# Converting float64 weights inside an attention and expert kernel: an integer sum in place of a float product

## The chip, the cores and the metric

The kernel runs on one core of one Trainium2 chip. The metric is device time in microseconds (us). Before the change three runs gave 2444.08, 2444.11 and 2446.53 us; the median is 2444.11 us.

## What is computed

Top-k attention over 4 batches, 8 heads, 576 rows of 64 (the 32 largest scores of a row are kept), then a bilinear layer, then eight experts weighted by a gate that is normalised eight times. The part that matters here is the layer in the middle:

```python
def _moe_ref(x, w1, w2, w3, w_out):
    a = x @ w1
    b = x @ w2
    h = a * b @ w3
    return (h @ w_out).astype(np.float32)
```

Its four weights are drawn as float32 and divided by a numpy float64 scalar, so they reach the kernel as 64-bit floats. The chip's engines work on 32-bit numbers, so the kernel has to make float32 out of float64 bits itself: sign, exponent and the first mantissa bits lie in the top 16-bit word, the rest in the words below it.

## The kernel before

**The attention stage** is a loop of 72 steps (`for s in range(NS + 6)`, L615). In step s VectorE finds the 32 largest scores of two rows of tiles (`st_topk`, L214): four rounds of MAX8 (L221) with three rounds of MATCH_REPLACE8 (L227) between. ScalarE evicts scores of step s+1 (L202), masks and exponentiates step s-1 (L234, L246), and evicts the transposed probabilities and the attention output of step s-2 (L270, L304). GpSimd normalises (L261), TensorE does the products. Every engine runs its instructions in the order in which the program wrote them, so one that waits holds up all that stands behind it on its engine.

**The conversion** of the four weights is woven into the first 23 steps: 40 pieces of 128x512 numbers, 8 of `w_out`, then 16 of `w3` with 8 of `w1` among them, then 8 of `w2`. A piece goes through `cv_run` (L341). `run_cv` (L556) calls it at two places in a step, after the second transposition and at the end of the step. There ScalarE computes two candidates `ca` and `cb` from the top word (L351, L352), and, for `w_out` alone, scales the low 32-bit word (L356). VectorE's part is put into `dve_q`, from which `st_topk` takes one entry at each of its seven slots (`dve_slot`) in the next step: `c1` chooses between the candidates and writes the top half of the float (L359, into `Q`), `c2` keeps sign and exponent (L363), `c3` multiplies these by the low word (L373; for `w_out` GpSimd does it, L371). GpSimd then adds `Q` and the product (L376, L378). For `w1` and `w2` the sum is split into a high and a low part for the later products: `hi` on ScalarE (L334), `lo` on GpSimd (L335), by `cv_flush`, in the middle of the same step.

**The raw pieces** come by DMA from SP's queue into `raw`, which has three buffers (`RB`). `cv_next` (L327) issues the load of piece n+3 as soon as the program has written `c3` of piece n, since no later instruction reads the raw words.

**w_out and w3** are multiplied with each other first: TensorE transposes a `w3` piece (L442), ScalarE copies it out (`w3t`, L443), TensorE multiplies it with `wo` (`wps`, L451), ScalarE evicts (L453). These items follow in the step after the piece was converted.

**After the `w1` pieces** (`NCA` = 32 of them done) the pools are closed and new ones opened for `w2` (`wt_close`, L422); `cb` then has one buffer instead of two. When all 40 pieces are done, `moe1_pool` opens the buffers of the middle layer and its products (L492, L510) are dealt out over the steps up to the next batch: step 37 for the first batch. The number of steps left sets how many products a step gets (`per`, L625). After the 72 steps come the experts (L690 on), where TensorE is busy throughout.

Of the kernel before, what the change touches and what calls it, by code (L numbers as in the profile page):

```python
# [7 lines left out]
F32 = mybir.dt.float32  # L8
F32R = mybir.dt.float32r
U16 = mybir.dt.uint16  # L10
U32 = mybir.dt.uint32
AF = mybir.ActivationFunctionType
ALU = mybir.AluOpType
AX = mybir.AxisListType
# [3 lines left out]
def kernel(  # L18
# [14 lines left out]
    nc = tc.nc  # L33
# [15 lines left out]
    scale = 1.0 / float(D) ** 0.5  # L49
# [65 lines left out]
    split = {}  # L115

    def copy(dst, src, eng):
        if eng is None:
            nc.scalar.activation(dst, src, AF.Copy)
        else:  # L120
            eng.tensor_copy(dst, src)

    def prep_split(p, nm, eng=nc.gpsimd):
        src = nat.pop((nm, p))
        hl = ap1.tile([128, 2 * R + 1, 2, D], F32R, name=f"{nm}hl", tag=f"{nm}hl")
        nc.scalar.activation(hl[:, :, 0, :], src, AF.Copy)
        eng.tensor_tensor(hl[:, :, 1, :], src, hl[:, :, 0, :].bitcast(F32), ALU.subtract)
# [58 lines left out]
    def st_scores(st, j):  # L186
# [13 lines left out]
        if j == 0:  # L200
            s_sb[st] = ap1.tile([128, 2, S], F32, name="s_sb", tag="s_sb", bufs=3)
        nc.scalar.activation(s_sb[st][:, j].rearrange("p (a b) -> p a b", a=2), ps[:, :, 0:SH], AF.Copy,  # L202
                             scale=scale)

    dve_q = []
# [25 lines left out]
    def st_over(st, j):  # L231

        x = s_sb[st][:, j]
        nc.scalar.activation(x, x, AF.Prelu, bias=tkv[st][:, j, TOPK - 1:TOPK], scale=-1.0, alpha=2.0 ** -100)  # L234

# [5 lines left out]
    def st_exp(st, j):  # L241
        if j == 0:
            e_sb[st] = ap1.tile([128, 2, S], F32, name="e_sb", tag="e_sb", bufs=2)
            rden[st] = ap1.tile([128, 2], F32, name="rden", tag="rden", bufs=2)
        rd = rden[st]
        nc.scalar.activation(e_sb[st][:, j], s_sb[st][:, j], AF.Exp, bias=nbias[st][:, j:j + 1],  # L246
                             scale=-(2.0 ** 100), accum_out=rd[:, j:j + 1])
        if j:
            nc.scalar.activation(rd, rd, AF.Identity, bias=eps)
            nbias.pop(st)  # L250
# [56 lines left out]
    CW = 512  # L307
    RB = 3
# [4 lines left out]
    cv = {"p": cvx.enter_context(tc.tile_pool(name="cv", bufs=1, side="left")), "n": 0}  # L313
    w3r = {}
    raws = {}
    gsc = G.rearrange("p f t -> p (f t)")
# [3 lines left out]
    nc.gpsimd.memset(gsc[:, 0:2 * CW], 0.0)  # L320

    def cv_load(key, src):
        t = cv["p"].tile([128, 4 * CW + 4], U16, name="raw", tag="raw", bufs=RB)
        nc.sync.dma_start(t[:, 1:4 * CW + 1], src.bitcast(U16))
        raws[key] = t

    def cv_next(n):  # L327
        if n < len(cvs) and not n - 3 < NCA <= n:
            cvs[n][1]()

    cv_post = []

    def hi_lo(w, hi, lo):
        nc.scalar.activation(hi, w, AF.Copy)  # L334
        nc.gpsimd.tensor_tensor(lo, w, hi.bitcast(F32), ALU.subtract)  # L335
# [5 lines left out]
    def cv_run(key, dst, done=None):  # L341
        t = raws.pop(key)
        pos = cpos[0]
        y = t[:, 4:4 * CW + 4].rearrange("p (n f) -> p n f", f=4)[:, :, 0]
        rest = t.bitcast(U32)[:, 0:2 * CW].rearrange("p (n f) -> p n f", f=2)[:, :, 1]
        n, m = cv["n"] % 2, cv["n"] % 3
        cv["n"] += 1
        Q = gsc[:, CW * n:CW * n + CW]
        ca = gsc[:, CW * (2 + m):CW * (3 + m)]
        cb = cv["p"].tile([128, CW], F32, name="cb", tag="cb", bufs=1 if "w2" in m1p else 2)  # L350
        nc.scalar.activation(ca, y, AF.Relu, bias=cbias[:, 0:1], scale=8.0)  # L351
        nc.scalar.activation(cb, y, AF.Identity, bias=cbias[:, 1:2], scale=8.0)  # L352

        off = key[0] == "o"
        if off:
            nc.scalar.activation(rest.bitcast(F32), rest, AF.Copy, scale=2.0 ** -36)  # L356

        def c1():
            nc.vector.scalar_tensor_tensor(Q.bitcast(U16).rearrange("p (n f) -> p n f", f=2)[:, :, 1],  # L359
                                           ca, 32768.0, cb, op0=ALU.min, op1=ALU.max)  # L360

        def c2():
            nc.vector.tensor_scalar(ca.bitcast(U32), Q.bitcast(U32), 0xff800000, None, op0=ALU.bitwise_and)  # L363

        def c23():
            c2()
            c3()

        def c3():
            if off:  # L370
                nc.gpsimd.tensor_tensor(ca, rest.bitcast(F32), ca, ALU.mult)  # L371
            else:
                nc.vector.scalar_tensor_tensor(ca, rest, 2.0 ** -36, ca, op0=ALU.mult, op1=ALU.mult)  # L373
            cv_next(pos + 3)
            if key[0] in ("o", "3"):
                nc.gpsimd.tensor_tensor(dst(), Q, ca, ALU.add)  # L376
            else:
                nc.gpsimd.tensor_tensor(ca, Q, ca, ALU.add)  # L378
                cv_post.append(lambda: hi_lo(ca, *dst()))
            if done is not None:  # L380
                done()

        dve_q.extend([c1, c23] if off else [c1, c2, c3])

    def cv_list():
        r = []

        def add(key, src, dst, done=None):
            r.append((key, lambda: cv_load(key, src), lambda: cv_run(key, dst, done)))

        def w3dst(i, hf):
            w3r[i, hf] = wtp.tile([128, CW], F32, name="w3r", tag="w3r", bufs=4)
            return w3r[i, hf]

        def wdst(n, c, sl):
            hi, lo = (w1h, w1l) if n == 0 else m1p["w2"]
            return hi[:, c, sl], lo[:, c, sl]

        for i in range(FC):
            add(("o", i), w_out[128 * i:128 * i + 128, :], lambda i=i: wo[:, i])  # L400
        def add3(i, hf):
            add(("3", i, hf), w3[128 * i:128 * i + 128, CW * hf:CW * hf + CW], lambda: w3dst(i, hf),
                lambda: later(1, w_items(i, hf)))

        def add12(n, c, hf):
            sl = slice(CW * hf, CW * hf + CW)
            add((n, c, hf), (w1, w2)[n][128 * c:128 * c + 128, sl], lambda: wdst(n, c, sl))

        k3 = [(i, hf) for i in range(FC) for hf in range(2)]
        k1 = [(c, hf) for c in range(KD) for hf in range(2)]  # L410
        for n, k in enumerate(k3):
            add3(*k)
            if n % 3 == 2:
                add12(0, *k1.pop(0))
        for k in k1:
            add12(0, *k)
        for c in range(KD):
            for hf in range(2):
                add12(1, c, hf)
        return r  # L420

    def wt_close():  # L422
        cvx.close()
        wt.close()
        m1p["w2p"] = wab.enter_context(tc.tile_pool(name="w2p", bufs=1, side="left", reuse_waits="tile"))
        m1p["w2"] = [m1p["w2p"].tile([128, KD, F1], F32R, name=n) for n in ("w2h", "w2l")]
        cvx2 = ExitStack()
        cv["p"] = cvx2.enter_context(tc.tile_pool(name="cv2", bufs=1, side="left", reuse_waits="tile"))
        m1p["cvx2"] = cvx2

    m1p = {}
# [123 lines left out]

    def run_cv():  # L556
        n = cpos[0]
        if n >= len(cvs) or sum(f is not None for f in dve_q) > 3:
            return
        key, _, fn = cvs[n]  # L560
        if key[0] == "3" and len(w3r) >= 4 and list(w3r)[-4] not in w3done:
            return
        if n == NCA and "w2" not in m1p:
            if dve_q or cv_post or fill or later_q or (FC - 1, 1) not in w3done:
                return
            wt_close()
            for i in range(3):
                cvs[n + i][1]()
            return
        if key not in raws:  # L570
            return
        fn()
        cpos[0] = n + 1
    load_pair(0)
    cvs = cv_list()
    cpos = [0]
    NCA = len(cvs) - FC
# [17 lines left out]
    st_scores(0, 0)  # L595
    st_scores(0, 1)
    run_cv()
    prep_group(0, "q", 2)
    run_cv()
    first = [9 * p // 2 for p in range(NPAIR + 1)]  # L600
    prep, loads = {}, {}
# [13 lines left out]
    for s in range(NS + 6):  # L615
# [52 lines left out]
        if 0 < s and cpos[0] < len(cvs):  # L668
            run_cv()
# [376 lines left out]
```

## Time and profile before

| | |
|---|---|
| median of three runs | 2444.11 us |
| span of the profiled execution | 2442.0 us |
| what lies around the span (median less span) | 2.1 us |
| TensorE busy | 2288.3 us, 94% of the span |
| VectorE busy | 1958.9 us, 80% |
| ScalarE busy | 1256.2 us, 51% |
| GpSimd busy | 1343.2 us, 55% |
| chain that ended last | TensorE 80%, VectorE 11%, ScalarE 5%, GpSimd 2% |

The page lists the time of no single execution beside its profile, so the span stands for it and the 2.1 us are taken as fixed. Shares over the whole span mix two halves: up to about 800 us the attention stage, after it the experts. In a timeline a row gives the start, the length, the engine, the line, what is written and read, and in brackets how long the engine had been idle and who ended that. PE is TensorE, PEld its weight load, DVE is VectorE, ACT is ScalarE, POOL is GpSimd, SP issues the DMAs. An ACT or DVE instruction begins while the end of the one before still drains, so the time that one takes of its engine is the distance to the next start, not its length.

### The profile page before, as it was taken

How to read it: one execution, taken by the hardware profiler on the slowest of the kernel's cores; microseconds unless marked ns; L12 is line 12 of the kernel's file. 1: busy time of each engine (PE TensorE's matmuls, PEld its weight loads, DVE VectorE, ACT ScalarE, POOL GpSimd, SP SyncE). 2: the span in 40 equal slices, each digit the busy share in tenths (PEclk: the TensorE clock that was granted, in tenths of full speed). 3: DMA queues.
4: the chain of work that ended last, by engine and by line, in shares of the span. 5: the costliest groups of instructions: out<-in, count | busy, mean ns of one | idle time of the engine just before them, and what ended most of it. 6: DMA issues, size and time to landing. Idle time of an engine off the chain costs nothing.

```text
span 2442.0 us, 37866 instructions
## 1 busy us (share of the span) xinstructions
PE 2288.3 (94%) x13061; PEld 2002.0 (82%) x13061; DVE 1958.9 (80%) x3560; ACT 1256.2 (51%) x2725; POOL 1343.2 (55%) x1377
## 2 busy tenths in 40 slices
PE   4677699899899999999999999999999999999999
PEld 3454489789788888889999988888888899999998
DVE  7998999999999228887777778777777777777776
ACT  6686777777777333444443444443444443444342
POOL 4534443233332125686666668666666666666664
PEclk7898789999999999999999999999999999999999
DMA  4332211111110132222222232222222322222221
GB/s 132 111 97 77 85 35 44 41 45 36 49 32 11 46 116 66 74 82 69 65 67 70 70 100 83 67 63 70 69 69 62 95 70 69 69 63 68 70 70 52
DMA packets 173296, 166.59 MB, mean 68 GB/s; under 512 B 19632, under 2 KB 137392, under 8 KB 173104
## 3 DMA queue, kind: packets, MB, share of 16 engines
q1 hardware_dynamic: 173104, 164.17, 22.4%
q8 instruction: 103, 1.69, 0.3%
q14 instruction: 89, 0.73, 0.1%
HBM read 145.24 MB, written 9.44 MB: 63 GB/s over the span
## 4 chain that ended last, share of the span: by engine, by line
PE 80%; DVE 11%; ACT 5%; POOL 2%; issue 2%; DMA 1%; SPq 0%; POOLq 0%; DVEq 0%; ACTq 0%
PE y L933 31%; PE l1ps L866 27%; PE abps L492 8%; PE x2ps L510 4%; DVE tkv L221 4%; DVE tk L227 3%; PE xps L300 3%; PE sps L198 2%; PE tps L267 2%; PE wps L451 1%; DVE G L359 1%; PE pt L137 1%; ACT e_sb L246 1%; ACT et L270 1%; ACT s_sb L202 1%
## 5 line engine op out<-in xcount | busy, mean ns | idle before, releaser
L730 POOL TENSOR_TENSOR wal<-ws,wah 128x256 fp32r<-128x256 f32 x665 | 553.9, 840 | 482.7 <-ACT wah L729 471.7
L946 DVE SCALAR_TENSOR_TENSOR acc<-y,P,acc 128x512 f32<-128x512 f32 x540 | 402.4, 745 | 215.0 <-PE y L933 214.0
L729 ACT ACTIVATE wah<-ws 128x256 fp32r<-128x256 f32 x672 | 276.3, 413 | 521.2 <-PE l1ps L866 514.9
L933 PE MATMUL y<-wbh,hh 128*128 128x512 f32 x1152 | 456.3, 396 | 4.5 <-ACT hh L887 4.5
L933 PE MATMUL y<-wbl,hh 128*128 128x512 f32 x1152 | 454.6, 395 | 0.0
L933 PE MATMUL y<-wbh,hl 128*128 128x512 f32 x1152 | 449.1, 390 | 1.9 <-DVE hl L890 1.4
L723 DVE TENSOR_TENSOR ws<-ws 128x256 f32<-128x256 f32 x384 | 319.0, 832 | 2.4 <-DMA ws<-in_moe_w_dram 1.8
L221 DVE MAX8 tkv<-tk 128x8 f32<-128x576 f32 x432 | 305.8, 752 | 0.0
L866 PE MATMUL l1ps<-xo0h,wah 128*128 128x384 f32 x896 | 304.6, 340 | 0.0
L866 PE MATMUL l1ps<-xo0h,wal 128*128 128x384 f32 x896 | 302.7, 338 | 0.0
L866 PE MATMUL l1ps<-xo0l,wah 128*128 128x384 f32 x896 | 302.7, 338 | 0.0
L933 PEld LDWEIGHTS y<-wbl,hh 128*128 128x128 f32 x1152 | 216.0, 188 | 52.7
L887 ACT ACTIVATE hh<-u 128x384 fp32r<-128x384 f32 x192 | 100.9, 525 | 297.0 <-DVE u L879 297.0
L933 PEld LDWEIGHTS y<-wbh,hl 128*128 128x128 f32 x1152 | 216.8, 188 | 30.3 <-DVE hl L890 5.8
L933 PEld LDWEIGHTS y<-wbh,hh 128*128 128x128 f32 x1152 | 216.6, 188 | 28.9 <-ACT hh L887 6.2
L738 POOL TENSOR_TENSOR wbl<-ws,wbh 128x1024 fp32r<-128x1024 f32 x96 | 231.8, 2414 | 12.5 <-ACT wbh L737 4.3
L227 DVE MATCH_REPLACE8 tk<-tkv,tk 128x576 f32<-128x576 f32 x288 | 212.4, 747 | 0.0
L866 PEld LDWEIGHTS l1ps<-xo0l,wah 128*128 128x128 f32 x896 | 169.2, 189 | 16.3
L866 PEld LDWEIGHTS l1ps<-xo0h,wah 128*128 128x128 f32 x896 | 168.9, 189 | 16.0 <-DVE hl L890 0.9
L501 POOL TENSOR_TENSOR G<-a_sb 128x256 f32<-128x256 f32 (+1 forms) x64 | 52.3, 817 | 227.4 <-ACT a_sb L497 211.6
L866 PEld LDWEIGHTS l1ps<-xo0h,wal 128*128 128x128 f32 x896 | 168.7, 188 | 0.0
L879 DVE TENSOR_TENSOR u<-l1ps,u 128x384 f32<-128x384 f32 x288 | 157.2, 546 | 4.8 <-PE l1ps L866 3.0
(146 smaller groups left out, 4912.2 us busy)
## 6 DMA issues: line engine op xcount, KB each, us to landing
ws<-in_moe_w_dram SPq DMA_DIRECT2D x384, 128.0 KB, 2.3
ws<-in_moe_w_dram SPq DMA_DIRECT2D x96, 512.0 KB, 3.5
raw<-in_moe_w_dram SPq DMA_DIRECT2D x32, 512.0 KB, 3.7
kst<-kst SPq DMA_DIRECT2D x30, 288.0 KB, 4.0
xr<-x2s SPq DMA_DIRECT2D x12, 384.0 KB, 3.6
xr<-x2s SPq DMA_DIRECT2D x6, 768.0 KB, 4.7
kn<-in_k_dram SPq DMA_DIRECT2D x16, 256.0 KB, 2.7
qn<-in_q_dram SPq DMA_DIRECT2D x16, 256.0 KB, 2.8
```

Of the source, the lines that this page charges most:

```text
L221: nc.vector.max(vt[:, j, 8 * r:8 * r + 8], a[j] if r else s[j])
L227: nc.vector.match_replace(a[j], vt[:, j, 8 * r:8 * r + 8], a[j] if r else s[j], -3.0e38)
L492: nc.tensor.matmul(ps[:, 0:n], lhs[:, c, fs], rhs[:, c, 0:n], start=(c == 0 and j == 0), stop=(c == KD - 1 and j == 2))
L723: nc.vector.tensor_tensor(st[:, dst], st[:, x], st[:, y], op)
L729: nc.scalar.activation(hi, st[:, slot], AF.Copy)
L730: eng.tensor_tensor(lo, st[:, slot], hi.bitcast(F32), ALU.subtract)
L738: nc.gpsimd.tensor_tensor(lo, st, hi.bitcast(F32), ALU.subtract)
L866: nc.tensor.matmul(ps[:, 0:TH], lhs[:, c], rhs[:, slot, c], start=(k_ == 0), stop=(k_ == 3 * KH - 1))
L879: nc.vector.tensor_tensor(t[nm], ps, t[x], ALU.add)
L887: nc.scalar.activation(t["hh"][:, i, h], src, AF.Relu)
L933: nc.tensor.matmul(ps, lhs[:, m, h, o:o + 128], rhs[:, m], start=(k_ == 0), stop=(k_ == 5))
L946: nc.vector.scalar_tensor_tensor(a, ps, P[:, t, e:e + 1], a, op0=ALU.mult, op1=ALU.add)
```

## The change

The float32 bits are put together as integers. ScalarE rounds the low word of every piece to an int32 (scaled by 2^-13, written back over the raw words as `low`), VectorE makes the top half with `c1` alone, and GpSimd adds `Q` and `low` as int32. `c2` and `c3` go, and so does GpSimd's product for `w_out`. For `w1` and `w2` the sum is written back into the raw buffer, and `hi` and `lo` read it there; so `cv_next` now stands behind `lo` for these, and behind GpSimd's sum for the others. In the `w2` part `cb` has two buffers again, and `raw` two (`RB - 1`). The candidates `ca` have two buffers instead of three.

```diff
     def cv_next(pos):
-        if n < len(cvs) and not n - 3 < NCA <= n:
+        n = pos + (RB if pos < NCA else RB - 1)
+        if n < len(cvs) and not pos < NCA <= n:
             cvs[n][1]()
...
-        n, m = cv["n"] % 2, cv["n"] % 3
+        n = cv["n"] % 2
-        ca = gsc[:, CW * (2 + m):CW * (3 + m)]
-        cb = cv["p"].tile([128, CW], F32, name="cb", tag="cb", bufs=1 if "w2" in m1p else 2)
+        ca = gsc[:, CW * (2 + n):CW * (3 + n)]
+        cb = cv["p"].tile([128, CW], F32, name="cb", tag="cb", bufs=2)
...
-        off = key[0] == "o"
-        if off:
-            nc.scalar.activation(rest.bitcast(F32), rest, AF.Copy, scale=2.0 ** -36)
+        low = rest.bitcast(I32)
+        nc.scalar.activation(low, rest, AF.Copy, scale=2.0 ** -13)
+
+        def split():
+            hi_lo(rest.bitcast(F32), *dst())
+            cv_next(pos)
...
         def c1():
             nc.vector.scalar_tensor_tensor(Q.bitcast(U16)..., ca, 32768.0, cb, op0=ALU.min, op1=ALU.max)
-        def c2():
-            nc.vector.tensor_scalar(ca.bitcast(U32), Q.bitcast(U32), 0xff800000, None, op0=ALU.bitwise_and)
-        def c3():
-            if off:
-                nc.gpsimd.tensor_tensor(ca, rest.bitcast(F32), ca, ALU.mult)
-            else:
-                nc.vector.scalar_tensor_tensor(ca, rest, 2.0 ** -36, ca, op0=ALU.mult, op1=ALU.mult)
-            cv_next(pos + 3)
             if key[0] in ("o", "3"):
-                nc.gpsimd.tensor_tensor(dst(), Q, ca, ALU.add)
+                nc.gpsimd.tensor_tensor(dst().bitcast(I32), Q.bitcast(I32), low, ALU.add)
+                cv_next(pos)
             else:
-                nc.gpsimd.tensor_tensor(ca, Q, ca, ALU.add)
-                cv_post.append(lambda: hi_lo(ca, *dst()))
+                nc.gpsimd.tensor_tensor(low, Q.bitcast(I32), low, ALU.add)
+                cv_post.append(split)
-        dve_q.extend([c1, c23] if off else [c1, c2, c3])
+        dve_q.append(c1)
...
     def run_cv():
-        if n >= len(cvs) or sum(f is not None for f in dve_q) > 3:
+        if n >= len(cvs) or len(dve_q) > 1:
...
-            for i in range(3):
+            for i in range(RB - 1):
                 cvs[n + i][1]()
```

How the instructions stand. On VectorE, in step 6, which converts two pieces (`tkv` are the maxima, `tk` the score tiles, `s_sb` the fresh scores; line numbers of the changed kernel are a few higher); before:

```order
120 L359 SCALAR_TENSOR_TENSOR G<-G,cb 128x512
121 L227 MATCH_REPLACE tk_769<-tkv,s_sb 128x576
122 L227 MATCH_REPLACE tk_770<-tkv,s_sb 128x576
123 L363 TENSOR_SCALAR G<-G 128x512
124 L221 MAX tkv<-tk_769 128x8
125 L221 MAX tkv<-tk_770 128x8
126 L373 SCALAR_TENSOR_TENSOR G<-raw,G 128x512
127 L227 MATCH_REPLACE tk_769<-tkv,tk_769 128x576
128 L227 MATCH_REPLACE tk_770<-tkv,tk_770 128x576
129 L359 SCALAR_TENSOR_TENSOR G<-G,cb 128x512
```

and on the same engine in the same step after the change:

```order
103 L222 MAX tkv<-s_sb 128x8
104 L256 RECIPROCAL rden<-rden 128x2
105 L222 MAX tkv<-s_sb 128x8
106 L364 SCALAR_TENSOR_TENSOR G<-G,cb 128x512
107 L228 MATCH_REPLACE tk_752<-tkv,s_sb 128x576
108 L228 MATCH_REPLACE tk_753<-tkv,s_sb 128x576
109 L364 SCALAR_TENSOR_TENSOR G<-G,cb 128x512
110 L222 MAX tkv<-tk_752 128x8
111 L222 MAX tkv<-tk_753 128x8
112 L228 MATCH_REPLACE tk_752<-tkv,tk_752 128x576
```

The second piece's `c1` moves from the fourth slot to the second, where the first piece's `c2` stood.

On ScalarE, at the middle and the end of step 18, the first that splits `w2` pieces (`et`, `xT` belong to the attention), before:

```order
312 L270 ACTIVATE et<-tps 128x640
313 L351 ACTIVATE G<-raw,cbias 128x512
314 L352 ACTIVATE cb<-raw,cbias 128x512
315 L334 ACTIVATE w2h<-G 128x512 x2
316 L304 ACTIVATE xT<-xps 128x128
317 L351 ACTIVATE G<-raw,cbias 128x512
318 L352 ACTIVATE cb<-raw,cbias 128x512
```

and after the change, from the same place on:

```order
338 L271 ACTIVATE et<-tps 128x640
339 L337 ACTIVATE w2h<-raw 128x512 x2
340 L305 ACTIVATE xT<-xps 128x128
341 L354 ACTIVATE G<-raw,cbias 128x512
342 L355 ACTIVATE cb<-raw,cbias 128x512
343 L357 ACTIVATE raw<-raw 128x512
344 L235 ACTIVATE s_sb<-s_sb,tkv 128x576 x2
```

With two raw buffers one piece instead of two is begun in this step, and its three instructions stand close behind the `hi` rows that read the raw words of the two before it. The `w2` pieces are chosen on VectorE in steps 18 to 21, two a step, before, and in steps 18 to 22, as 2, 1, 2, 1 and 2, after. Up to step 17 the pieces stand in the same steps in both kernels, and TensorE's rows are the same.

## Rows read from the trace of the kernel before

**Rows 1.** The page's first line.
```profile
span 2442.0 us, 37866 instructions
```
**Rows 2.** Timeline of VectorE in step 5, which converts two pieces.
```profile
77.64 0.74 DVE L221 MAX8 tkv<-s_sb 128x8 f32<-128x576 f32 x1
...
81.29 0.41 DVE L363 TENSOR_SCALAR G<-G 128x512 uint32<-128x512 uint32 x1
81.62 1.41 DVE L221 MAX8 tkv<-tk 128x8 f32<-128x576 f32 x2
82.95 0.67 DVE L373 SCALAR_TENSOR_TENSOR G<-raw,G 128x512 f32<-128x512 uint32 x1
83.54 0.08 DVE L227 MATCH_VALUE_LOAD tk<-tkv,tk 128x8 f32 x1
...
85.00 0.74 DVE L359 SCALAR_TENSOR_TENSOR G<-G,cb 128x512 uint16<-128x512 f32 x1
...
90.67 0.74 DVE L221 MAX8 tkv<-s_sb 128x8 f32<-128x576 f32 x1
```
**Rows 3.** Timeline of VectorE in a step without conversion.
```profile
636.85 0.76 DVE L221 MAX8 tkv<-s_sb 128x8 f32<-128x576 f32 x1
...
646.56 0.75 DVE L221 MAX8 tkv<-s_sb 128x8 f32<-128x576 f32 x1
```
**Rows 4.** Stretches: length, busy PE, PEld, DVE, ACT, POOL (instructions), clock, DMA, GB/s.
```profile
77.09:249.98 172.89, 130.82 (x735) 82.65 (x736) 159.68 (x325) 122.74 (x245) 70.48 (x72) 0.89 0.30 94
261.38:313.80 52.42, 33.05 (x164) 25.65 (x164) 52.42 (x104) 37.84 (x76) 24.45 (x24) 0.58 0.23 68
322.69:462.21 139.52, 138.92 (x1142) 125.90 (x1141) 136.97 (x296) 106.70 (x241) 46.81 (x66) 0.99 0.15 42
```
**Rows 5.** Waits of ScalarE, 77 to 250 us: us in total, times, longest.
```profile
ACT et L270 <- PE tps L268: 19.6, 8, 4.9
ACT xT L304 <- PE xps L300: 19.0, 8, 6.1
ACT G L351 <- POOL w1l L335: 5.4, 3, 4.7
...
ACT s_sb L234 <- DVE tkv L221: 1.1, 1, 1.1
```
**Rows 6.** Waits of VectorE, 77 to 250 us.
```profile
DVE G L359 <- ACT cb L352: 9.0, 5, 2.6
```
**Rows 7.** Timeline of ScalarE, end of step 7.
```profile
115.54 0.59 ACT L443 ACTIVATE w3t<-pt 128x512 f32<-128x512 f32 x1
121.09 0.28 ACT L304 ACTIVATE xT<-xps 128x128 f32<-128x128 f32 x1 [4.95 <-PE xps L300]
```
**Rows 8.** Timeline of TensorE, the same place.
```profile
116.19 3.61 PE L451 MATMUL wps<-wo,w3t 128*128 128x512 f32 x4 [3.87 <-ACT w3t L443]
```
**Rows 9.** ScalarE's scaling of the low word, by line: ns min/median/max.
```profile
L356 ACT ACTIVATE raw<-raw x8: 646/662/713, 17.9 to 61.4; 128x512 f32<-128x512 uint32 x8
```
**Rows 10.** Timeline of ScalarE in steps 6 and 8, from the split on.
```profile
104.13 0.62 ACT L334 ACTIVATE w1h<-G 128x512 fp32r<-128x512 f32 x1
104.64 0.59 ACT L453 ACTIVATE W<-wps 128x512 f32<-128x512 f32 x1
...
106.13 0.77 ACT L351 ACTIVATE G<-raw,cbias 128x512 f32<-128x512 uint16 x1 [0.18 <-POOL w1l L335]
...
137.25 0.28 ACT L304 ACTIVATE xT<-xps 128x128 f32<-128x128 f32 x1 [0.45 <-PE xps L300]
```
**Rows 11.** GpSimd's low part by line, and the raw loads' time to landing.
```profile
L335 POOL TENSOR_TENSOR w1l<-G,w1h x8: 1256/1275/1368, 104.8 to 249.2; 128x512 fp32r<-128x512 f32 x8
...
DMA to landing us min/median/max: 3.2/3.7/5.4
```
**Rows 12.** Timeline of VectorE and of GpSimd in step 19.
```profile
272.77 1.75 DVE L359 SCALAR_TENSOR_TENSOR G<-G,cb 128x512 uint16<-128x512 f32 x1
...
271.43 2.50 POOL L335 TENSOR_TENSOR w2l<-G,w2h 128x512 fp32r<-128x512 f32 x2
```

More of the change, by code (lines that the diff above doesn't have):

```diff
@@ L11 @@
 U32 = mybir.dt.uint32
+I32 = mybir.dt.int32
 AF = mybir.ActivationFunctionType
@@ L322, in cv_load, with cv_next @@
     def cv_load(key, src):
-        t = cv["p"].tile([128, 4 * CW + 4], U16, name="raw", tag="raw", bufs=RB)
+        t = cv["p"].tile([128, 4 * CW + 4], U16, name="raw", tag="raw",
+                         bufs=RB - 1 if "w2" in m1p else RB)
         nc.sync.dma_start(t[:, 1:4 * CW + 1], src.bitcast(U16))
         raws[key] = t
-    def cv_next(n):
-        if n < len(cvs) and not n - 3 < NCA <= n:
+    def cv_next(pos):
+        n = pos + (RB if pos < NCA else RB - 1)
+        if n < len(cvs) and not pos < NCA <= n:
             cvs[n][1]()
@@ L360, in c1 @@
                                            ca, 32768.0, cb, op0=ALU.min, op1=ALU.max)
-        def c2():
-            nc.vector.tensor_scalar(ca.bitcast(U32), Q.bitcast(U32), 0xff800000, None, op0=ALU.bitwise_and)
-        def c23():
-            c2()
-            c3()
-        def c3():
-            if off:
-                nc.gpsimd.tensor_tensor(ca, rest.bitcast(F32), ca, ALU.mult)
-            else:
-                nc.vector.scalar_tensor_tensor(ca, rest, 2.0 ** -36, ca, op0=ALU.mult, op1=ALU.mult)
-            cv_next(pos + 3)
-            if key[0] in ("o", "3"):
-                nc.gpsimd.tensor_tensor(dst(), Q, ca, ALU.add)
-            else:
-                nc.gpsimd.tensor_tensor(ca, Q, ca, ALU.add)
-                cv_post.append(lambda: hi_lo(ca, *dst()))
+            if key[0] in ("o", "3"):
+                nc.gpsimd.tensor_tensor(dst().bitcast(I32), Q.bitcast(I32), low, ALU.add)
+                cv_next(pos)
+            else:
+                nc.gpsimd.tensor_tensor(low, Q.bitcast(I32), low, ALU.add)
+                cv_post.append(split)
             if done is not None:
                 done()
-        dve_q.extend([c1, c23] if off else [c1, c2, c3])
+        dve_q.append(c1)
     def cv_list():
```

## The prediction

> **What bounds the kernel now.** I began with the span [rows 1] and then asked the attention stage, in which the conversion sits, step by step. The first look is VectorE's timeline. A step that converts two pieces runs from 77.64 to 90.67, 13.03 us [rows 2]; a step that converts nothing takes 9.71 us [rows 3]. The reader is to see that VectorE goes from row to row without a gap, and that the difference of 3.3 us is the conversion. Read alone this says: VectorE is the bound, so take work off it.
>
> The second look is at stretches [rows 4]. From step 5 to step 17 (77.09 to 249.98) ScalarE was busy 122.74 of 172.89 us. That seems slack. The third look, who waited for whom, says otherwise: of ScalarE's 50 us of idle time there only 1.1 us was a wait for VectorE [rows 5]. Nearly all is for TensorE, in two forms of eight times each, up to 6.1 us. And VectorE itself waited 9.0 us for ScalarE's candidates `cb` [rows 6]. So ScalarE runs behind VectorE through these steps, and its waits are not VectorE's doing.
>
> The fourth look shows what they are. ScalarE copies `w3t` out at 115.54 and then has nothing to do until 121.09, when it gets `xps` [rows 7]. TensorE meanwhile had sat idle for 3.87 us, waiting for exactly that copy, and then took 3.61 us for four products [rows 8]. ScalarE and TensorE hand the work to and fro; when one works on this chain the other stands. In steps 5 to 16 this chain, 173 us for 12 steps, sets the pace as much as VectorE does. A faster VectorE cannot shorten it; more ScalarE work lengthens it.
>
> **The change part by part.**
>
> *VectorE.* `c2` takes 0.33 us (81.29 to 81.62) and `c3` 0.59 (82.95 to 83.54) [rows 2]. 40 x 0.33 + 32 x 0.59 = 32.1 us less. That is the whole prize, and it is only paid where VectorE sets the end. In steps 0 to 4 it nearly does. There mostly `w_out` pieces are converted, which lose `c2` alone, and the first two pieces wait for their loads. I take -1 us, between -4 and 0.
>
> *The second `c1` earlier.* It moves to the second slot. The fourth is 7.36 us into a step (85.00), the second 3.65 us (81.29) [rows 2]. Its candidates come from the end of ScalarE's step before, so VectorE now tolerates 3.7 us less of ScalarE's lag. It costs nothing of its own; it is what makes VectorE wait for the chain in every step rather than in five.
>
> *ScalarE.* One rounding more for each `w3`, `w1` and `w2` piece. The nearest row is the scaling of the same words, 0.66 us long [rows 9]. ScalarE's instructions overlap by 0.1 (a `hi` of 0.62 begins 0.51 before the next) [rows 10], so I take 0.56; an int32 output could change that, I allow 0.4 to 0.8. Between step 5 and step 16 there are 21 of them, 11.8 us, on the chain. Some fall into a wait for TensorE in which TensorE isn't waiting for ScalarE, such as the 0.45 us at 137.25 [rows 10]; I count five such places and 2.5 us in all, between 0 and 5. **+9.3 us.**
>
> *The raw buffer is held longer.* For a `w1` piece the load of the piece three later now waits for `lo`. From the start of `hi` that is 0.62 [rows 10], then 1.27 for `lo` and 3.7 for the landing [rows 11]: 5.6 us. The `w1` pieces of steps 6, 8, 10, 12 and 14 are each the first of their pair, so the piece three later is the one ScalarE takes at the end of the same step. In step 6 it gets there 2.0 us after `hi` (104.13 to 106.13) [rows 10]. It will stand 3.6 us. The same for steps 8 and 10: 10.8 us. In step 12 ScalarE already waits 4.7 us at this place, for a candidate's buffer that GpSimd still reads [rows 5]; two early `c1` free that, so 3.6 takes the place of 4.7, -1.1. In step 14 the wait of 6.1 us for `xps` [rows 5] covers it. **+9.7 us**, between 0 (loads land early) and 15. On SP the loads behind such a wait are those of later pairs' keys, queries and values, needed steps later; nothing.
>
> *GpSimd.* One product less for `w_out`, the additions as integers. No row shows an integer addition there; at half or at twice the 1.27 us of the nearest row, `lo` [rows 11], it would still be done well before ScalarE, some 6 us into its step, reaches `hi`. Nothing.
>
> So the chain reaches step 18 later by -1 + 9.3 + 9.7 = 18 us.
>
> *Steps 18 to 22, `w2`.* Now two raw buffers, and each step's last piece is loaded into the buffer that the `hi` rows just before it have to leave. ScalarE's own work from step 18's start to step 22's was 37.84 us of 52.42 [rows 4]. After: six roundings more, two `hi` fewer by step 22, 37.84 + 6 x 0.56 - 2 x 0.51 = 40.2 us. In each of the four steps it stands for the refill: 5.6 us from `hi`, less what it still does meanwhile, 1.2 us with two `hi` and 0.7 with one, so 4.4 or 4.9, twice each, 18.6 us. Together 58.8, 6.4 more. At the end VectorE gains: it began step 23 at 322.69, 8.9 us after that stretch. Now the last `c1` starts 0.6 us before the stretch ends, and 9.71 + 2 x 0.64 - 3.65 = 7.3 us of its step are left, so 6.7 us, 2.2 less (a `c1` of 0.74 takes 0.64). **+4.2 us**, between -10 (no refill wait) and +7.
>
> *One step later.* The last piece is finished in step 22, so the middle layer's products begin in step 24 instead of 23 and still end at step 37: 13 steps for the work of 14. TensorE was busy 138.92 of 139.52 us there [rows 4], so a step is 9.9 us and has no room. About half of it belongs to the layer; that half has to go elsewhere. Bounds 0 and 5; **+4 us**, near the upper one since TensorE is full.
>
> Sum: 18 + 4.2 + 4 = 26.2 us. On the span 2468.2; with 2.1 us around it, which puts the profiled execution at the median of the three runs, 2470.3, say **2470 us**.
>
> **A rule to weigh.** A `c1` of 0.74 us took 1.75 at 272.77 while GpSimd worked from 271.43 to 273.93 [rows 12]. It seems to have stood until GpSimd's instruction ended. The Trainium skill, in SBUF — State Buffer, Who interferes with whom, says that a VectorE instruction with two SBUF inputs contends with a GpSimd instruction that reads SBUF, and that the later one fully blocks. The trace agrees, with 1.0 us. My sum has none of it, since VectorE waits for ScalarE anyway.
>
> **Rivals.**
>
> *A: VectorE is the bound after all and ScalarE keeps up.* For it: no gaps in most steps [rows 2]. The price is the whole 32.1 us, less 4 for the later start: 2444.1 - 28.1 = 2416 us. It decides if ScalarE's chain shrinks by a quarter when VectorE runs ahead. Against it: ScalarE's work alone, 122.7 + 21 x 0.56 = 134.5 us, would have to go through 12 steps of VectorE of 9.71 + 1.28, 132 us, without a single wait. Chance 0.07.
>
> *B: as A, but the second `c1` is blocked.* It now comes when GpSimd adds the first piece. By the 1.0 us of rows 12, in 18 steps with two pieces, up to 18 us are given back, half of that if GpSimd has got through half its addition: 2425 us. The rule of the Trainium skill above, in SBUF — State Buffer, would make this, not A, the case. Chance 0.06.
>
> *C: the loads come in time.* SP, GpSimd and the DMA answer faster than 5.6 us, or ScalarE gets there later. Then the roundings count, the buffer waits of 5.4 us [rows 5] go, and steps 18 to 22 are VectorE's: 8 pieces x 0.92, and three blocked `c1` of 1.0, -10.4. -1 + 9.3 - 5.4 - 10.4 + 4 = -3.5: 2441 us, no change. Against it: landing never took under 3.2 us [rows 11]. Chance 0.12.
>
> *D: TensorE slows as well.* While it waits its granted clock falls: 0.89 on average in steps 5 to 16, 0.58 in the `w2` stretch [rows 4]. Of its two levels, 1.2 and 2.4 GHz, the lower would make products last twice as long; four products that took 3.61 us after an idle time of 3.87 [rows 8] would then have been 1.8. If longer waits put seven more handovers there, 7 x 1.8 = 12.6 us: 2483 us. Chance 0.15.
>
> **How the numbers follow.** The forecast has 0.60. Its own range, from the bounds of the roundings, the refills and the later start, is 2452 to 2484. A measurement of this kernel can tell about 0.2% from no change, 4.9 us: 2439.2 to 2449.0 is the same. Faster: A, B and a little of C, 0.14. Same: the rest of C and the forecast's lowest edge, 0.12. Slower: 0.74. The range reaches down to take in C and up to take in D: 2437 to 2486; A, B and the far ends, 2 in 10, are left out.
>
> **What would show it.** ScalarE's waits: a new kind, `ca` on the DMA of `raw`, of 3 to 5 us, some seven times from step 6 on, with L270's and L304's waits for TensorE much as before. VectorE's waits for `cb` far above 9 us over the same steps. Step 18 starting some 15 us later, step 23 some 22 later, the step of 9.71 unchanged where nothing is converted, the experts shifted and not stretched. I am wrong if VectorE's steps 5 to 15 take about 11 us each (A), if ScalarE never waits for `raw` (C), or if the products of L451 get slower (D).

## The result, and the profile after the change

The changed kernel took 2477.39 us (median of 4 runs, 2475.37 to 2478.79) against 2445.30 us for the kernel before (4 runs): 1.0129 times as long, 95% interval 1.0115 to 1.0143, 32 us slower. The profiled execution took 2477.46 us, 1.8 us of it around the span. The page's first lines:

```profile
span 2475.7 us, 37823 instructions
...
PE 2299.4 (93%) x13061; PEld 2010.7 (81%) x13061; DVE 1924.0 (78%) x3488; ACT 1274.4 (51%) x2757; POOL 1334.2 (54%) x1369
```

VectorE is busy 34.9 us less than before (1958.9), and the span is 33.6 us longer (unrounded) [rows 1]. The groups by line, up to 400 us, say what became of the time (busy, mean ns of one, idle time ahead of them):

```profile
L364 DVE SCALAR_TENSOR_TENSOR G<-G,cb 128x512 uint16<-128x512 f32 x40 | 35.0, 876 | 72.7 <-ACT cb L355 72.6
L354 ACT ACTIVATE G<-raw,cbias 128x512 f32<-128x512 uint16 x40 | 30.6, 764 | 37.1 <-DMA raw<-in_moe_w_dram 32.6 <-DMA raw<-in_moe_w_out_dram 4.5
...
L357 ACT ACTIVATE raw<-raw 128x512 int32<-128x512 uint32 x40 | 26.7, 668 | 0.0
L370 POOL TENSOR_TENSOR raw<-G,raw 128x512 int32<-128x512 int32 x16 | 20.6, 1290 | 21.7 <-DVE G L364 18.8 <-ACT raw L357 2.1 <-ACT s_sb L235 0.8
```

and the first of them in the kernel before:

```profile
L359 DVE SCALAR_TENSOR_TENSOR G<-G,cb 128x512 uint16<-128x512 f32 x40 | 34.9, 873 | 12.2 <-ACT cb L352 12.2
```

The 40 `c1` now stand for 72.6 us and wait for ScalarE's `cb`; before it was 12.2. VectorE saved 34.9 us of work and got 60.4 us of waiting for it. The second line after the change shows a wait that the kernel before hardly had: ScalarE's `ca` on the load of `raw`, 32.6 us for `w3`, `w1` and `w2`.

The stretches, cut by ScalarE's steps as before (steps 5 to 16, steps 18 to 21; the last is VectorE's steps 23 to 36), answer to [rows 4]:

```profile
76.60:271.75 195.15, 140.03 (x736) 87.71 (x737) 139.22 (x284) 134.22 (x266) 68.23 (x72) 0.84 0.26 77
282.59:342.14 59.55, 29.80 (x173) 23.40 (x173) 43.86 (x91) 39.87 (x80) 25.67 (x27) 0.71 0.25 78
349.30:493.66 144.36, 141.54 (x1129) 128.13 (x1126) 137.74 (x296) 106.00 (x238) 51.81 (x68) 0.97 0.14 39
```

They are longer by 22.3, 7.1 and 4.8 us. In the first, ScalarE's own work grew by 11.5 us and VectorE's busy time fell from 159.68 to 139.22.

ScalarE's waits from 77 to 272 us, which answer to [rows 5], and then those from 283 to 342:

```profile
ACT et L271 <- PE tps L269: 21.4, 9, 4.9
ACT xT L305 <- PE xps L301: 19.3, 5, 5.0
ACT G L354 <- DMA raw<-in_moe_w_dram: 15.8, 4, 4.7
...
ACT s_sb L235 <- DVE tkv L222: 0.4, 1, 0.4
...
ACT G L354 <- DMA raw<-in_moe_w_dram: 16.8, 4, 5.6
```

The two waits for TensorE are what they were (19.6 and 19.0); so is that for VectorE, close to nothing. New are the eight waits for `raw`, four and four. VectorE's waits over the first stretch stood at 9.0 us in five [rows 6]:

```profile
DVE G L364 <- ACT cb L355: 51.9, 14, 7.6
```

One of the eight from close by: ScalarE in step 6, from the split on (start, length), which answers to [rows 10],

```profile
104.16 0.68 ACT L357 ACTIVATE raw<-raw 128x512 int32<-128x512 uint32 x1
104.72 0.66 ACT L337 ACTIVATE w1h<-raw 128x512 fp32r<-128x512 f32 x1
...
106.24 0.34 ACT L296 ACTIVATE xT<-xps 128x64 f32<-128x64 f32 x2
111.26 0.75 ACT L354 ACTIVATE G<-raw,cbias 128x512 f32<-128x512 uint16 x1 [4.68 <-DMA raw<-in_moe_w_dram]
```

and the chain of waits over the same microseconds:

```profile
105.46 0.13 POOL w1l L338
...
106.78 4.40 DMA raw<-in_moe_w_dram
...
111.26 0.75 ACT G L354
112.01 0.64 ACT cb L355
```

`hi` begins at 104.72, `lo` at 105.46 (it takes 1.29), SP issues the load at 106.78, the words are there at 111.18, and `ca` starts at 111.26: 6.54 us after `hi`. VectorE's second `c1` of this step stands 6.58 us for it, until 113.12. In steps 8, 10 and 12 the same distance is 5.97, 6.24 and 6.22 us.

To compare kernels I use the start of each of VectorE's steps (its first MAX8 on `s_sb`) less that in the profile of the kernel before. Numbers are in us; "end" is the span, unrounded.

| kernel | 5 | 8 | 9 | 12 | 18 | 22 | 23 | 37 | 50 | end |
|---|---|---|---|---|---|---|---|---|---|---|
| changed | -0.5 | 3.2 | 8.5 | 17.0 | 20.2 | 21.0 | 26.6 | 31.5 | 33.1 | 33.6 |
| e1, both sums in `ca` | -0.3 | -0.1 | 4.5 | 5.9 | 5.7 | 0.0 | 0.0 | -1.4 | -1.4 | -0.6 |
| e9, `w1` sum in `ca` | 0.6 | 0.7 | 4.5 | 5.4 | 2.2 | 2.6 | 8.0 | 12.9 | 14.5 | 17.1 |
| e10, `w2` sum in `ca` | -0.3 | 3.5 | 9.5 | 17.7 | 21.0 | 15.4 | 15.4 | 13.9 | 13.9 | 15.9 |
| e7, rounding on GpSimd | -0.3 | -2.7 | 0.9 | 0.8 | -4.6 | -10.5 | -10.5 | -11.3 | -11.3 | -9.8 |
| e8, rounding on VectorE | 0.0 | -2.1 | 0.3 | -4.4 | -11.3 | -17.3 | -17.3 | -20.2 | -19.3 | -18.3 |
| e5, before, layer later | 0.6 | 0.0 | 0.8 | 1.4 | 1.6 | 1.6 | 1.6 | 8.0 | 9.4 | 11.4 |

e1 and e9 are the same program up to step 17; so are the changed kernel and e10, but for e10's third buffer for `ca`. At step 18 their profiles differ by 3.5 and 0.8 us, and the profiled execution of e7 was its longest (2434.29 us), that of e8 its shortest (2425.82): a shift read from one profile is good to some 4 or 5 us. After step 50 the changed kernel loses 0.5 us more, the others 0.8 to 2.7: the experts are moved and hardly stretched.

### The profile page after: what moved, and what is told of

It reads as the page before. It is cut to its first block, busy times and chain, and to the rows that moved or that the text cites. A ratio compares the mean times of both kernels' runs of the same rounds, so it can differ in the third digit from the quotient of the medians.

```text
span 2475.7 us, 37823 instructions
## 1 busy us (share of the span) xinstructions
PE 2299.4 (93%) x13061; PEld 2010.7 (81%) x13061; DVE 1924.0 (78%) x3488; ACT 1274.4 (51%) x2757; POOL 1334.2 (54%) x1369
## 4 chain that ended last, share of the span: by engine, by line
PE 77%; ACT 8%; DVE 7%; issue 3%; POOL 2%; DMA 2%; SPq 0%; POOLq 0%; ACTq 0%; DVEq 0%
PE y L925 31%; PE l1ps L858 27%; PE abps L484 7%; PE x2ps L502 4%; DVE tkv L222 3%; DVE tk L228 2%; PE xps L301 2%; PE sps L199 2%; PE tps L268 2%; DMA raw<-in_moe_w_dram 1%; PE wps L443 1%; ACT e_sb L247 1%; ACT et L271 1%; ACT s_sb L203 1%; ACT G L354 1%
## 5 line engine op out<-in xcount | busy, mean ns | idle before, releaser
L199 PE MATMUL sps<-kst,qst 128*128 128x288 f32 x640 | 140.2, 351 | 54.6 <-ACT s_sb L203 54.2
```

Source lines behind the costliest of these rows:

```text
L199: nc.tensor.matmul(ps[:, e, 0:SH], lhs, kst[p, part][:, hh, SH * e:SH * e + SH], start=(n == 0), stop=(n == len(terms) - 1))
```

## The experiments

The theory: ScalarE's chain sets the pace, and the change puts two things on it, the roundings and the wait for a buffer that is held until `lo`. The rivals: VectorE is the bound in other places (A, B), the loads are in time (C), TensorE's clock (D).

**e1: the buffer given back early.** The sum of `w1` and `w2` goes into `ca` (three again), so that `hi` and `lo` don't read the raw words, and the next load is issued right behind the sum:

```diff
-        ca = gsc[:, CW * (2 + n):CW * (3 + n)]
+        ca = gsc[:, CW * (2 + m):CW * (3 + m)]
...
-            hi_lo(rest.bitcast(F32), *dst())
-            cv_next(pos)
+            hi_lo(ca, *dst())
...
-                nc.gpsimd.tensor_tensor(low, Q.bitcast(I32), low, ALU.add)
+                nc.gpsimd.tensor_tensor(ca.bitcast(I32), Q.bitcast(I32), low, ALU.add)
+                cv_next(pos)
```

> The changed kernel, but for w1 and w2 the integer sum goes into the candidate's buffer ca (three of them again) and the load of the next piece is issued behind the sum, not behind lo. The roundings stay. Theory (ScalarE's chain with TensorE, plus refill waits): the waits of ScalarE for raw, 15.8 us in steps 6 to 12 and 16.8 in the w2 steps, go; w2 takes 4 steps again and the middle layer starts one step earlier (6.5 us). About 30 to 37 us faster than the changed kernel: 2440 to 2448 us, at most a little under the kernel before, since the roundings remain. Rival (the roundings, or TensorE at its lower clock, made the loss): the refill waits turn into other waits, over 2460 us.

Measured: 2443.22 us, 0.9985 times the kernel before (0.9975 to 0.9995). That is 34 us under the changed kernel: more than its whole loss hangs on this. ScalarE's waits from 77 to 255 us:

```profile
ACT et L271 <- PE tps L269: 21.0, 8, 4.9
ACT xT L305 <- PE xps L301: 20.3, 5, 5.9
...
ACT G L354 <- POOL w1l L338: 0.8, 3, 0.3
```

There is no wait for `raw` in this list, and those for TensorE are the same as in both kernels. Yet VectorE, with 32 us less to do, came out only 2.7 us ahead:

```profile
DVE G L363 <- ACT cb L355: 29.9, 12, 6.9
DVE G L363 <- POOL e_sb L262: 3.8, 2, 2.1
```

It still waits 29.9 us for ScalarE, which carries the roundings. The rest of the experiments take these two parts further apart.

**e9 and e10: one of the two weights at a time.** As e1, but with the sum in `ca` for `w1` alone (e9) or for `w2` alone (e10); `key[0]` is 0 for `w1` and 1 for `w2`, and e10 has 0 in the place of the 1:

```diff
-            hi_lo(rest.bitcast(F32), *dst())
-            cv_next(pos)
+            hi_lo(rest.bitcast(F32) if key[0] == 1 else ca, *dst())
+            if key[0] == 1:
+                cv_next(pos)
```

> The changed kernel, but the sum of w1 pieces alone goes into ca and their next load is issued behind the sum; w2 pieces stay as changed. If the refill waits of steps 6 to 14 and those of steps 18 to 22 are separate terms that add: VectorE's step 18 starts 5 to 8 us later than in the kernel before (20.2 in the changed kernel, 5.7 with both sums in ca), ScalarE still waits some 16 us for raw in the w2 steps, step 23 starts 6 us later than that, and the middle layer's later start adds 6 or 7: 2461 to 2467 us. Rival: the second group of waits is only the echo of the first (ScalarE enters step 18 late); then step 23 is no later than step 18 and the time is 2448 to 2454.

> The changed kernel, but the sum of w2 pieces alone goes into ca and their next load is issued behind the sum; w1 pieces stay as changed. If the terms are separate: step 18 starts about 20 us later than before, the w2 steps have no refill wait and give 5 to 6 us back, the middle layer begins in step 23 as before, so nothing is added there: 2456 to 2462 us. Rival: the lateness of step 18 is made up in the w2 steps, where VectorE is the bound: 2443 to 2450.

Measured: e9 2461.19 us, 1.0060 (1.0045 to 1.0075); e10 2457.78 us, 1.0045 (1.0028 to 1.0061). Both fall into the range of separate terms. ScalarE's waits for `raw` in e9, from 262 to 365 us,

```profile
ACT G L354 <- DMA raw<-in_moe_w_dram: 16.5, 4, 5.4
```

and in e10, from 77 to 265 us:

```profile
ACT G L354 <- DMA raw<-in_moe_w_dram: 16.8, 4, 4.6
```

Each kernel kept the group of waits whose weight was left as changed, at its full size (16.8 and 15.8 with both). In e9 step 18 starts only 2.2 us late, lower than I had put it, and step 23 still loses 5.8 us to it, the layer another 6.5; so the second group is no echo of the first. In e10 step 18 is 21.0 us late, and the `w2` steps give 5.6 back. e10 also has the third `ca`, which the changed kernel lacks: up to step 18 it gains nothing by it (21.0 beside 20.2). Against the kernel before on the same chip, the four medians stand at -2.7 (e1), +14.4 (e9), +11.0 (e10) and +32.1 (changed). Holding `w1`'s buffers costs 13.7 or 17.7 us, depending on which pair is compared, holding `w2`'s 17.1 or 21.1, the layer's later start included.

**e5: the middle layer one step later, in the kernel before.** Nothing else is changed:

```diff
-        if s >= marks[0] and "p" not in m1p and cpos[0] == len(cvs) and not dve_q and not cv_post:
+        if s >= 23 and "p" not in m1p and cpos[0] == len(cvs) and not dve_q and not cv_post:
```

> The kernel before, but the middle layer's buffers are opened one step later (step 23 instead of 22); nothing of the conversion is changed. Theory (TensorE is full from step 23 to 36, so a step's share of products has to go elsewhere): 4 to 7 us slower than the kernel before, with the first half of the 72 steps unchanged. Rival (VectorE sets these steps too): no change within 1 us.

Measured: 2452.52 us, 1.0031 (1.0018 to 1.0044), 7.5 us slower, a little over the 4 to 7. By the table 6.4 us are lost between steps 23 and 37 and 1.4 more up to step 50; in the changed kernel 4.9 and 1.6. Stretches of VectorE's step 23 and of its steps 24 to 36, in the kernel before,

```profile
322.69:332.39 9.70, 9.53 (x82) 8.62 (x81) 9.70 (x22) 8.02 (x19) 2.29 (x5) 0.92 0.26 63
332.39:462.21 129.82, 129.39 (x1063) 117.28 (x1062) 127.27 (x275) 98.68 (x223) 44.52 (x62) 1.00 0.14 40
```

and in e5:

```profile
324.31:334.01 9.70, 6.11 (x45) 4.24 (x43) 9.70 (x22) 8.13 (x17) 4.03 (x4) 0.85 0.17 33
334.01:470.23 136.22, 135.57 (x1092) 123.78 (x1093) 128.25 (x275) 98.73 (x224) 45.21 (x62) 0.98 0.14 39
```

In step 23 TensorE does 3.4 us less (6.11 for 9.53). In steps 24 to 36, where it is full in both, it is busy for 6.2 us more, and it is VectorE that waits there (7.8 us for ScalarE's rows, 2.2 before). More of the layer's products stand in these steps: e5 has 64 of each of the six kinds that L492 issues, before it was 56 of three kinds and 60 of the others, 36 more at the same 295 to 320 ns.

Moved work is only a part of it. Over steps 23 to 36 together TensorE was busy for 138.92 us before and for 141.68 in e5, so 3.4 of the 6.2 us came over from step 23 and 2.8 are new. The granted clock can account for these. In step 23 of e5 TensorE had little to do (0.24 us of work from 330 to 332 us), and the clock, at 1.00 from 327 to 332, was 0.71 from 332 to 334. The next step begins with 5.5 us at 0.50, the lower of the two levels (1.2 GHz); at half speed that costs 2.7 us, by my estimate. No run moves the clock alone. In e5,

```profile
334.01:339.50 5.49, 5.38 (x32) 5.03 (x32) 5.49 (x14) 3.00 (x8) 1.66 (x3) 0.50 0.18 55
334.12 2.40 PE L300 MATMUL xps<-et,vn 128*64 128x128 f32 x18 [0.91 <-ACT et L270]
```

and in the kernel before as many of the same products, at the start of step 23 (0.86 from 324 to 325 us, then 1.00), and its step 24, which ran at 1.00:

```profile
324.19 1.34 PE L300 MATMUL xps<-et,vn 128*64 128x128 f32 x18 [0.17 <-ACT et L270]
332.39:342.09 9.70, 9.70 (x93) 9.40 (x92) 9.70 (x22) 7.46 (x18) 2.56 (x6) 1.00 0.01 3
```

The changed kernel does the same at this place: the 18 products take 2.39 us at 358.00, and the clock is 0.50 from 357 to 362 us. After step 37 another 1.4 us are lost; in e5 and in the changed kernel step 38 takes 10.2 us instead of 9.7.

**e2: without the rounding.** Zeros are added in place of the rounded low word for `w3`, `w1` and `w2`:

```diff
-        nc.scalar.activation(low, rest, AF.Copy, scale=2.0 ** -13)
+        if key[0] == "o":
+            nc.scalar.activation(low, rest, AF.Copy, scale=2.0 ** -13)
+        add = low if key[0] == "o" else gsc[:, 4 * CW:5 * CW].bitcast(I32)
```

> The changed kernel without ScalarE's rounding for w3, w1 and w2: their low words are left out of the sum (zeros are added instead), all else is as in the changed kernel. Theory: 21 roundings of 0.56 us less on the chain, less the few that were hidden: 7 to 13 us faster than the changed kernel, 2464 to 2470 us, still 20 us slower than the kernel before, and the refill waits of ScalarE stay or grow a little. Rival (ScalarE's extra work is the whole loss): back to 2445 to 2450.

Measured: 2453.34 us, 1.0032 (1.0019 to 1.0045): neither. The edit did more than I meant. With no rounding, nothing that comes after ScalarE's candidates reads a `w3` piece's raw words, and its buffer came free earlier too: in step 6 the load that ScalarE waits for was issued at 103.7 us, as soon as `cb` of a `w3` piece was done, and not behind `lo`, which ended at 105.6. The waits for `raw`, from 77 to 265 us and from 262 to 360 us:

```profile
ACT G L355 <- DMA raw<-in_moe_w_dram: 4.3, 2, 2.6
...
ACT G L355 <- DMA raw<-in_moe_w_dram: 16.3, 4, 5.8
```

So 11.5 of the 15.8 us went with the roundings, and only the `w2` group stayed. The run mixes both terms and prices neither; e7 and e8 do it.

**e3: VectorE's relief alone.** The kernel before without `c2` and without VectorE's `c3`:

```diff
-            nc.vector.tensor_scalar(ca.bitcast(U32), Q.bitcast(U32), 0xff800000, None, op0=ALU.bitwise_and)
+            pass
...
-                nc.vector.scalar_tensor_tensor(ca, rest, 2.0 ** -36, ca, op0=ALU.mult, op1=ALU.mult)
+                pass
```

> The kernel before without c2 everywhere and without VectorE's c3 (sign and exponent are not masked and the low word is left out for w3, w1, w2); c1 and GpSimd's sums stay in their slots. This is the whole prize, 32 us of VectorE's work, with nothing given for it. Theory: ScalarE's chain sets steps 5 to 16, so only the w2 steps, steps 0 to 4 and the end of step 16 gain: 10 to 20 us faster than the kernel before, 2425 to 2435. Rival (VectorE is the bound): 32 us or more, under 2414.

Measured: 2425.98 us, 0.9919 (0.9900 to 0.9937). That is 20 us for the 32 removed, with no cost of the change paid yet. By the starts of the steps it gains 5.7 us from step 5 to step 18, where it drops 23 `c2` and 23 `c3` (21.2 us by the prediction's prices), and 9.3 from there to step 23, where it drops 8 of each (7.4 us). In the steps of the chain most of the relief became waits of VectorE, for `cb` (9.0 us before) and for the reciprocal's input, from 77 to 245 us:

```profile
DVE G L359 <- ACT cb L352: 22.1, 10, 6.1
DVE rden L255 <- ACT rden L249: 7.0, 4, 3.1
```

**e4: ScalarE's load alone.** The kernel before with ScalarE's scaling for every piece; VectorE's `c3` then reads the scaled word:

```diff
-        if off:
+        if True:
             nc.scalar.activation(rest.bitcast(F32), rest, AF.Copy, scale=2.0 ** -36)
...
-                nc.vector.scalar_tensor_tensor(ca, rest, 2.0 ** -36, ca, op0=ALU.mult, op1=ALU.mult)
+                nc.vector.scalar_tensor_tensor(ca, rest.bitcast(F32), 1.0, ca, op0=ALU.mult, op1=ALU.mult)
```

> The kernel before with one ScalarE instruction more for each w3, w1 and w2 piece (it scales the low word, as w_out's pieces have it already); VectorE's c3 then reads the scaled word. VectorE's work and all slots are as before. Theory: the roundings' price alone, 7 to 12 us slower than the kernel before, 2452 to 2457. Rival (ScalarE's 49 us of idle time in those steps takes it in): no change, 2444 to 2447.

Measured: 2453.02 us, 1.0028 (1.0017 to 1.0039), 7.1 us slower. Its steps are 4.4 us late at step 18 and 4.5 at step 23, in a profile of one of its shorter executions (2449.20 us): 32 more instructions of 0.68 us cost this much even where VectorE has kept all its work.

**e6: the second `c1` in its old place.** The changed kernel with two empty slots between the pieces:

```diff
-        dve_q.append(c1)
+        dve_q.extend([c1, None, None])
```

(and `run_cv` counts the entries that are not empty).

> The changed kernel with the second piece's c1 back in the fourth slot of VectorE's step (two empty slots follow each c1). Theory (VectorE only waits for ScalarE's chain; the place of c1 sets where it waits, not how long the chain is): within 4 us of the changed kernel, 2473 to 2481, with VectorE's waits for cb cut by some 30 us of the 52 and other waits or none in their place. Rival (the early c1 is what costs): 10 us or more faster than the changed kernel.

Measured: 2474.93 us, 1.0118 (1.0103 to 1.0133). The interval overlaps with that of the changed kernel. VectorE's waits for `cb` fell only to 43.2 us, by 9 and not by the 30 that I expected, and those for the reciprocal's input rose to 13.3 (2.5 in the changed kernel): where VectorE stands in a step makes no difference while ScalarE is the one that it waits for.

**e7 and e8: the rounding taken off ScalarE.** Both are e1, with the rounding of `w3`, `w1` and `w2` elsewhere. In e7 it is done by GpSimd, from the same place in the program; in e8 by VectorE in the slot behind `c1`.

```diff
-        nc.scalar.activation(low, rest, AF.Copy, scale=2.0 ** -13)
+        if key[0] == "o":
+            nc.scalar.activation(low, rest, AF.Copy, scale=2.0 ** -13)
+        else:
+            nc.gpsimd.tensor_scalar(low, rest, 2.0 ** -13, None, op0=ALU.mult)
```

> The version with the sum in ca, with the rounding of w3, w1 and w2 done by GpSimd instead of ScalarE. Theory: ScalarE's chain loses its roundings, 7 to 12 us faster than the version with the sum in ca: 2431 to 2437 us, under the kernel before by 0.3 to 0.6%; VectorE's waits for cb fall to about 22 us, as where c2 and c3 were left out. Rival (GpSimd, 2.5 us a step more, holds up its own normalising and the sums): ScalarE waits for GpSimd instead, no gain, 2441 us or more.

> The same with the rounding done by VectorE, in the slot behind c1; the second c1 then stands in the third slot. Theory: in steps 5 to 16 VectorE waits for ScalarE anyway (30 us in the version with the sum in ca), so the rounding is free there and costs 8 x 0.3 to 0.6 us in the w2 steps: 2431 to 2439 us. Rival (VectorE's own work counts): 2443 or more.

Measured: e7 2430.12 us, 0.9930 (0.9914 to 0.9947); e8 2431.86 us, 0.9939 (0.9924 to 0.9954). Both are faster than both kernels; between them the intervals tell nothing. e7 came out 0.9 us below the range that I had given. The rounding by line, in e7,

```profile
L360 POOL TENSOR_SCALAR raw<-raw 128x512 int32<-128x512 uint32 x32 | 51.1, 1598 | 15.4 <-DMA raw<-in_moe_w_dram 13.3
```

and in e8:

```profile
L372 DVE TENSOR_SCALAR raw<-raw 128x512 int32<-128x512 uint32 x32 | 15.3, 479 | 0.0
```

VectorE's wait for `cb` from 77 to 255 us, in e7,

```profile
DVE G L366 <- ACT cb L355: 25.0, 11, 6.3
```

and in e8:

```profile
DVE G L365 <- ACT cb L355: 13.3, 7, 3.9
```

GpSimd takes 1.60 us for what ScalarE does in 0.67, and it is the better place all the same: 51.1 us on an engine whose roundings nobody waits for (0.2 us of TensorE's weight loads in all) against 21 on the chain. The price is small: TensorE's waits for GpSimd's normalised scores, from 77 to 320 us, are 19.9 us for 14.8 in e1. VectorE, busy for 144 of 160 us in steps 5 to 16 of e8, was as good a place. In e7 step 18 starts 10.3 us earlier than in e1. Neither version shortens the chain between ScalarE and TensorE itself; that wasn't tried.

## Why the prediction was right

The time came out 7 us above the forecast and within its own range. By the steps of the prediction:

- **The bound.** Right. VectorE's relief alone was worth 20 of 32 us (e3), and of the 21.2 us that fell in steps 5 to 17 only 5.7. What it was worth inside the changed kernel no run prices. Rival A needed steps of about 11 us from 5 to 15; they took 16.2 on average (77.14 to 255.31 for 11 steps; before it was 14.0), and 14.9 in e1, where no wait for `raw` is left.
- **Steps 0 to 4:** -1 forecast, -0.5 measured.
- **ScalarE's roundings:** +9.3 forecast. ScalarE's work grew by 11.5 us against 11.8 counted, and taking it off moved step 18 by 10.3 (e1 to e7). Putting the like of it on in the kernel before moved it by 4.4 (e4), so the two runs put the price on either side of the forecast.
- **The raw buffer, steps 6 to 14:** the mechanism was right, its size a little low. Forecast were 3.6 us in steps 6, 8, 10 and 12, and nothing in 14; measured 4.68, 4.31, 4.39 and 2.39, and nothing. The latency from `hi` to `ca` was put at 5.6 and was 6.0 to 6.5: `lo` starts 0.74 after `hi` (0.62 assumed), and the load took 4.40 to land where the median of before, 3.7, had been taken [rows 11]. With the 5.4 us of [rows 5] that it would have saved otherwise, the hold was to cost 9.7 + 5.4 = 15.1 us; e1 and e9 against the changed kernel and e10 say 14.5 to 18.8 at step 18.
- **Step 18** was to start some 15 us later by one sentence and 18 by the sum; it was 20.2.
- **Steps 18 to 22:** +4.2 forecast, 26.6 - 20.2 = 6.4 measured. ScalarE's stretch was forecast at 58.8 us and took 59.55: 39.87 of work (40.2 forecast) and 16.8 of waiting for `raw` (18.6), with 2.7 for TensorE that I had not counted. Most of the difference lies at the edges: ScalarE entered step 18 4.0 us behind VectorE instead of 3.0, and 7.2 us were left at the end, not 6.7.
- **One step later:** mis-sized. "+4 us, near the upper one since TensorE is full", with a bound of 5, became 6.5 in the changed kernel (26.6 at step 23, 33.1 at step 50) and 7.5 in e5. "About half of it has to go elsewhere" was, if anything, too much for the work: 3.4 us of TensorE's 9.7 moved in e5. What the term left out is the granted clock, 0.50 at the start of step 24, where TensorE's time grew by another 2.8 us, and the steps after 37, which lose 1.4 to 1.6 us more.
- **The sum:** 26.2 forecast, 33.6 measured. The missing 7.4 us are 2.2 up to step 18, 2.2 in the `w2` steps, 2.5 for the layer and 0.5 in the experts; all four miss to the same side, so the sum did not come out by errors that cancel.
- **Rival B:** not decided, since VectorE waits anyway. A `c1` took 876 ns on average, 873 before. Where VectorE is less held up, the block is there: in e1's `w2` steps a `c1` took 1.29 and 1.22 us at 277.03 and 279.68, when GpSimd had begun an instruction before it (it worked from 276.45 to 279.44 and again from 279.56), beside 0.71 at 289.06, just ahead of GpSimd's next at 289.23. The rule of the Trainium skill (SBUF — State Buffer, Who interferes with whom), by which the later of the two stands, agrees with this.
- **Rival C** failed with the eight waits for `raw`. e1 is close to the program that C described, with the loads early, but without a late layer: 2441 us for C, or 2437 without the 4 us for the layer; 2443.2 measured.
- **Rival D:** the granted clock did fall in the conversion steps, 0.84 for 0.89, but rose in the `w2` steps, 0.71 for 0.58, and ScalarE's waits for TensorE stayed about as they were. The products of L443 (L451 before) took 730 ns each where they had taken 686; in e10 they took 723, in e1 and e9, whose loads are early here, 706 and 688. So the sign that the prediction had named for D came, in small: 128 x 44 = 5.6 us spread over the stretch, without a longer wait for them (ScalarE's for L443 came to 3.2 us in all, 3.8 before). How much of it lies on the chain no run tells. At a place that D did not name, the layer's first step, the lower clock is a part of the loss.

## What to carry to other kernels

A share of busy time of 71% on an engine says nothing about its slack: ask who it was waiting for, and whether that one was waiting for it. Work taken from the engine that looks full is only worth what the chain behind it allows, and work is best moved to an engine that nobody will wait for in these steps, even if it does it at less than half the speed. And an operation done in place prolongs the life of its buffer: count from the start of the last readers, here `hi` and `lo`, to the first use of the next load, here 6 us, and look who is standing there.

## What the runs showed that was not expected

- An integer addition on GpSimd costs what a float one does: 1.29 us for 128x512 int32, 1.28 before for float32.
- The same conversion of 128x512 from uint32 to int32 with a scale took 0.67 us on ScalarE, 0.48 on VectorE and 1.60 on GpSimd (means of 40, 32 and 32).
- A step left free of the layer, in front of a stretch in which TensorE is full, cost 6.5 to 7.8 us by step 50 (changed kernel, e5), though TensorE's busy time in the free step itself was only 3.4 us less. While TensorE waited there its granted clock fell, and the next step began at 0.50, where 18 products took 2.40 us; in the kernel before, at 0.86 to 1.00, as many took 1.34. Why the steps after 37 lose another 1.4 to 1.6 us is open.
